# Decay attention into a squared-gate MLP on one core: a planner that may choose the engine of eight kinds of instruction, and float32 scores of two heads on the two halves of the rows

## The chip, the cores and the metric

The kernel runs on one core of one Trainium2 chip. Its time is the device time of one execution in microseconds (us); lower is better. The engines are PE (TensorE, matrix products; PEld is its weight load), DVE (VectorE), ACT (ScalarE), POOL (GpSimd) and SP (SyncE, which here only issues DMAs).

## The reference

Attention with a decay for 8 batches, 8 heads, 576 positions and 64 channels a head, and then a two-layer MLP over the 4608 tokens (512 to 2048 to 512) whose gate is quadratic between -1 and 1 and linear above:

```python
scores = np.matmul(q, k.transpose(0, 1, 3, 2)) / np.sqrt(D)
cum = np.cumsum(np.log(np.clip(f, 0.0001, 1.0)), axis=-1)
decay = cum[:, :, :, None] - cum[:, :, None, :]
scores = np.where(causal, -1000000000.0, scores + decay)   # causal: above the diagonal
attn = np.exp(scores - np.max(scores, axis=-1, keepdims=True))
attn = attn / (np.sum(attn, axis=-1, keepdims=True) + 1e-09)
x = np.matmul(attn, v)           # then to [B * S, H * D]
h = x @ w_in
g = np.where(h >= 1, h, np.where(h <= -1, 0.0, (h + 1) ** 2 / 4))
out = g @ w_out
```

## The kernel before

**Attention** goes by jobs: one pair of heads of one batch, or for batch 0 a part of it (rows of blocks 0 and 1, then blocks 2 to 4), 36 jobs in all. A job takes the rows of its 576 positions in blocks of 128 (the fifth has 64; there the two heads share one tile, head 0 on partitions 0 to 63 and head 1 on 64 to 127). For each block and head POOL writes decay and mask into a row buffer `sdr` or `sd` (lines 884 and 888), PE writes the scores into one of three PSUM tiles `s`, DVE adds both and takes the minimum (906), ACT takes the exponential and its sum (915), POOL adds the small constant to the sum (921), DVE inverts it (927). Row buffers are a ring of four, and one `sd`.

The first 12 jobs (`p < NQK`) compute scores in float32: PE turns q and k (694), ACT copies them from PSUM to `qkT` (700 and 705), and PE multiplies (713). q is copied twice, head 0 into the upper 64 partitions of one tile and head 1 into the lower 64 of another, the other halves being zero, so that each product reads all 128 rows against the k of both heads. Each float32 product is two instructions in the trace. The first 8 jobs (`p < NPE`) also turn the probabilities on PE, with a diagonal of inverse sums (`pr<-ident`, 937) as the second operand (957, 963), copied from PSUM by ACT (973).

The later jobs split each number into a high and a low half of float16: the high half is written by ACT with a scale and the low half by DVE as a difference. So are q and k (`qs`, 759 and 763; 767 and 773), v (`vs`, 805 and 811), the probabilities (`pr`, 989 and 992). Probabilities and q, k are turned by DMA; the scores are 795, the products with v 846.

**The MLP** goes by 18 chunks of 256 tokens and 8 double blocks of the hidden width (144 steps). Per step: 24 or 48 products into a PSUM tile `ph` (1055), ACT adds and squares into `u` (1064, 1067), DVE bounds it (1068), ACT writes the high half of `g` (1071), DVE the low half (1074), PE multiplies both with the second weights into `po` (1082). After the last step ACT scales two `po` tiles into `ot` (1098) and issues their DMAs. There are three `ph`, two `u`, three `g`. The weights are split once, in the first 200 us; the low half of the first matrix is made by POOL (524, 527), of the second by DVE (531).

**The order of the work** is a plan. Each piece of work is recorded with an engine, an estimated time, what it reads and writes, and a priority. `plan` then walks through estimated time and gives each free engine its first ready piece by priority, granting buffers as it goes, and the pieces are written out in that order. On the chip every engine runs its own list strictly in order. `A`, `V`, `G` and `M` record work for ACT, DVE, POOL and PE, so that the engine of a piece is fixed where it is recorded. `od.hold` keeps job ji from starting before 100 + 27 (ji - 8) us of planned time.

Of the kernel before, what the change touches and what calls it, by code (L numbers as in the profile page):

```python
# [9 lines left out]
F32 = mybir.dt.float32  # L10
# [61 lines left out]
class Order:  # L72
# [3 lines left out]
    def __init__(self):  # L76
        self.ops = []
        self.last = {}
        self.readers = {}
# [3 lines left out]
    def op(self, eng, dur, emit, reads=(), writes=(), prio=0.0, size=0.0, mode=0):  # L83
        i = len(self.ops)
        deps = set()
        bufs = set()
# [7 lines left out]
        for x in list(reads) + list(writes):  # L94
            b = x[0] if isinstance(x, tuple) else x
            if isinstance(b, Buf):
                bufs.add(b)
# [14 lines left out]
    def plan(self):  # L112
# [15 lines left out]
        for i in range(n):  # L128
            if not missing[i]:
                waiting[ops[i][0]].append(i)  # L130
# [6 lines left out]
        while done < n:  # L137
# [5 lines left out]
            while again:  # L143
                again = False
                for eng, l in waiting.items():
# [4 lines left out]
                    for i in l:  # L150
                        if ready[i] > t + 1e-9:
                            continue
# [34 lines left out]
                    l.remove(i)  # L187
# [31 lines left out]
                    for j in follow[i]:  # L219
                        missing[j] -= 1  # L220
                        same = ops[j][0] == eng and not size
                        late = SLACK if ops[j][0] == "PE" else 0.0
                        ready[j] = max(ready[j], free[eng] if same else after + late)
                        if not missing[j]:
                            k = (ops[j][5], j)
                            w = waiting[ops[j][0]]
                            lo, hi = 0, len(w)
                            while lo < hi:
                                mid = (lo + hi) // 2
                                if (ops[w[mid]][5], w[mid]) < k:  # L230
                                    lo = mid + 1
                                else:
                                    hi = mid
                            w.insert(lo, j)
                            if ready[j] > t:
                                heapq.heappush(events, ready[j])
# [21 lines left out]
def kernel(  # L258
# [119 lines left out]

    def M(us, emit, reads=(), writes=(), prio=0.0, mode=0):
# [45 lines left out]
    for i in range(1):  # L425
        G(0.3, lambda i=i: nc.gpsimd.memset(sd4_pool.cands[i][1][:, S:SP], 0.0), [], ["sdz"], -7.0)
    early_qk = {
        c: t[:, 0:6 * S].bitcast(F32).rearrange("p (c s) -> p c s", c=3) for c, t in qkt_pool.aps.items()
    }
    for c, t in early_qk.items():  # L430
        for h in range(2):
            G(0.6, lambda t=t, h=h: nc.gpsimd.memset(t[64 - 64 * h:128 - 64 * h, h, :], 0.0), [], ["qz"], -8.5)
# [51 lines left out]
    def weight_split(i, prio):  # L484
# [29 lines left out]
        for j in range(2):  # L514
# [8 lines left out]
            if j == 0:  # L523
                G(1.4, lambda wf=wf, s=s: nc.gpsimd.tensor_scalar(
                    out=wf, in0=wf, scalar1=s, scalar2=0.0, op0=ALU.mult, op1=ALU.add
                ), [("sw", i)], key, prio)
                G(2.6, lambda wf=wf, hi=hi, lo=lo: nc.gpsimd.tensor_tensor(
                    out=lo, in0=wf, in1=hi, op=ALU.subtract
                ), [], key + [("pl", i, j)], prio)
            else:  # L530
                V(1024, lambda wf=wf, hi=hi, lo=lo, s=s: nc.vector.scalar_tensor_tensor(
                    out=lo, in0=wf, scalar=s, in1=hi, op0=ALU.mult, op1=ALU.subtract
                ), [("sw", i)], key + [("pl", i, j)], prio)
# [91 lines left out]
    def attention(ji):  # L625
# [47 lines left out]
        if p < NQK:  # L673
# [9 lines left out]
            for j in range(2):  # L683
                part, _, keys = x32[j]
                n_all = s1 - (0 if j else s0)
                for a0 in range(0, n_all, 384):
# [10 lines left out]
                    if j == 0:  # L697
                        for h in range(2):
                            rows = slice(64 * h, 64 * h + 64)
                            A(n, lambda rows=rows, h=h, n=n, a0=a0, pt=pt: nc.scalar.activation(  # L700
                                view()[rows, h, a0:a0 + n], pt.ap[rows, 0:n], AF.Copy
                            ), [pt, "qz"], [(qt, h, a0)], pq)
                            qtkeys[h].append((qt, h, a0))
                    else:
                        A(n, lambda n=n, a0=a0, pt=pt: nc.scalar.activation(
# [467 lines left out]
```

## Time and profile before

| | us |
|---|---|
| median of 3 runs (range) | 1134.03 (1130.76 to 1135.49) |
| profiled execution, own time | 1131.35 |
| its span | 1129.6 |
| PE busy in it | 1053.3 (93%) |
| DVE, ACT, POOL busy | 800.5 (71%), 796.7 (71%), 478.8 (42%) |
| mean granted clock of PE | 0.981 |

The span is the time from the first to the last instruction that the profile shows; 1.75 us of the execution lie outside it. Busy times of an engine overlap with those of the others. A busy PE need not be PE at its peak, since the ends of its products are modelled.

### The profile page before, as it was taken

The numbers are of one execution on the slowest core, as the hardware profiler recorded it, in microseconds if no ns is written. First come the engines' busy times: TensorE is split into PE (matmuls) and PEld (weight loads), VectorE is DVE, ScalarE is ACT, GpSimd is POOL, SyncE is SP. The second block draws the span as 40 slices with busy tenths as digits, with TensorE's granted clock in tenths as the row PEclk, the third lists the DMA queues.
The fourth block names the chain that finished last, engine by engine and source line by source line (L and its number), as shares of the span: only waits on it lengthen the run. The fifth ranks groups of instructions, "written<-read, shape, count | busy, mean of one in ns | idle before, by whom it ended". The sixth has DMA issues, their size and how long they took to land. (4 is left out here: it accounts for less than half of the span.)

```text
span 1129.6 us, 24707 instructions
## 1 busy us (share of the span) xinstructions
PE 1053.3 (93%) x8805; PEld 708.8 (63%) x8805; DVE 800.5 (71%) x2156; ACT 796.7 (71%) x1667; POOL 478.8 (42%) x873
## 2 busy tenths in 40 slices
PE   4689788999999999999999999999999999999998
PEld 2445555556665666666666666666666667676675
DVE  5795888878878887887778878788787873322322
ACT  4566776776888887878787877788787974444443
POOL 4868863354554444444543543445434640000000
PEclk9689998999999999999999999999999999999999
DMA  7844444567779788768896987789868662000000
GB/s 195 284 149 104 151 127 111 103 120 152 149 165 179 144 168 154 160 136 166 164 170 141 170 147 160 145 171 170 145 133 153 138 120 41 17 21 11 10 19 19
DMA packets 390619, 146.37 MB, mean 130 GB/s; under 512 B 367328, under 2 KB 368352, under 8 KB 390496
## 3 DMA queue, kind: packets, MB, share of 16 engines
q1 hardware_dynamic: 385312, 135.35, 59.3%
q10 hardware_dynamic: 5184, 9.44, 2.4%
q8 instruction: 69, 1.13, 0.4%
q14 instruction: 54, 0.44, 0.1%
HBM read 65.68 MB, written 9.58 MB: 67 GB/s over the span
## 5 line engine op out<-in xcount | busy, mean ns | idle before, releaser
L1055 PE MATMUL ph<-x,place 128*128 128x256 f16 (+3 forms) x4608 | 407.0, 247 | 4.5 <-DVE x L863 1.4
L1082 PE MATMUL po<-place,g 128*128 128x512 f16 x1728 | 403.8, 381 | 2.6 <-ACT g L1071 2.3
L1055 PEld LDWEIGHTS <-place 128*128 128x128 f16 x4608 | 355.7, 98 | 55.3 <-issue 8.4
L1082 PEld LDWEIGHTS <-g 128*128 128x128 f16 x1728 | 164.1, 98 | 185.7 <-issue 5.2
L884 POOL TENSOR_SCALAR sdr<-ck,sg,cqs 128x128 f32<-128x128 f32 (+1 forms) x192 | 162.2, 845 | 201.2 <-DVE pr L992 180.4
L1068 DVE SCALAR_TENSOR_TENSOR u<-ph,z,u 128x512 f32<-128x512 f32 x144 | 107.4, 746 | 128.6 <-ACT u L1067 127.2
L915 ACT ACTIVATE sdr<-sdr,nm 128x512 f32<-128x512 f32 (+3 forms) x246 | 135.4, 551 | 52.9 <-DVE nm L906 34.2
L1064 ACT ACTIVATE u<-ph,z 128x512 f32<-128x512 f32 x144 | 110.4, 767 | 79.2 <-PE ph L1055 77.6
L1074 DVE SCALAR_TENSOR_TENSOR g<-u,z,g 128x512 f16<-128x512 f32 x144 | 113.6, 789 | 40.6 <-ACT g L1071 40.0
L989 ACT ACTIVATE pr<-sdr,nm 128x128 f16<-128x128 f32 (+1 forms) x224 | 114.3, 550 | 38.7 <-issue 23.6
L1071 ACT ACTIVATE g<-u,z 128x512 f16<-128x512 f32 x144 | 103.1, 716 | 53.1 <-DVE u L1068 52.4
L992 DVE SCALAR_TENSOR_TENSOR pr<-sdr,nm,pr 128x128 f16<-128x128 f32 (+1 forms) x224 | 115.8, 551 | 4.9 <-ACT pr L989 4.6
L906 DVE CUSTOM_DVE_ANT_0 sdr<-s,sdr,sg 128x128 f32<-128x128 f32 (+1 forms) x192 | 101.7, 541 | 22.2 <-POOL sdr L888 20.4
L795 PE MATMUL s<-qkT 128*128 128x128 f16 (+5 forms) x576 | 92.8, 297 | 11.2 <-DVE nm L906 6.7
L888 POOL TENSOR_SCALAR_AFFINE_SELECT sdr<-sdr 128x128 f32<-128x128 f32 x246 | 91.6, 372 | 18.1
L1067 ACT ACTIVATE u<-u 128x512 f32<-128x512 f32 x144 | 90.6, 629 | 4.2
L921 POOL TENSOR_SCALAR nm<-nm 128x2 f32<-128x2 f32 (+1 forms) x160 | 41.0, 256 | 93.8 <-ACT sdr L915 62.0
L846 PEld LDWEIGHTS <-vs 128*64 128x64 f16 x1176 | 58.6, 110 | 29.1 <-issue 23.8
L846 PE MATMUL s<-pT,vs 128*64 128x320 f16 (+4 forms) x1176 | 68.1, 263 | 9.1 <-DVE nm L906 5.9
L713 PE MATMUL s<-qkT 128*128 128x128 f32 (+5 forms) x192 | 64.4, 484 | 7.6 <-DVE nm L906 6.9
L795 PEld LDWEIGHTS <-qkT 128*128 128x128 f16 (+1 forms) x576 | 42.6, 101 | 42.5 <-issue 21.9
L884 POOL TENSOR_SCALAR sd<-ck,sg,cqs 64x576 f32<-64x576 f32 x48 | 42.2, 879 | 50.3 <-DVE pr L992 46.3
(138 smaller groups left out, 1129.3 us busy)
## 6 DMA issues: line engine op xcount, KB each, us to landing
ck<-cum_d SPq DMA_DIRECT2D x62, 288.0 KB, 3.7
out_dram<-ot ACTq DMA_DIRECT2D x36, 256.0 KB, 3.1
v<-in_v_dram SPq DMA_DIRECT2D x64, 128.0 KB, 3.2
qk<-in_k_dram SPq DMA_DIRECT2D x64, 128.0 KB, 3.0
qkT<-qkT SPq DMA_DIRECT2D x48, 160.0 KB, 3.5
qk<-in_q_dram SPq DMA_DIRECT2D x56, 128.0 KB, 3.1
place<-in_moe_w_in_dram SPq DMA_DIRECT2D x10, 512.0 KB, 4.9
place<-in_moe_w_out_dram SPq DMA_DIRECT2D x8, 512.0 KB, 6.3
```

The source lines that it names most:

```text
L795: nc.tensor.matmul(sp[p0:p1, 0:c1 - c0], lhsT=tq[:, h, q0 - s0:q0 - s0 + p1 - p0], rhs=tk[:, h, c0:c1], start=(c == 0), stop=(c == 1),)
L846: nc.tensor.matmul(av.ap[64 * h:64 * h + 64, c0:n], lhsT=vs.ap[:, vl, h, t, :], rhs=pT.ap[:, t, pl, h, c0:n], start=(t == 0 and pi == 0), ...
L884: nc.gpsimd.tensor_scalar(out=sd.ap[p0:p1, 0:wid], in0=cks[h].ap[p0:p1, 0:wid], scalar1=ns if p < NQK else ns[p0:p1], scalar2=cqs()[p0:p1, ...
L915: A(wid, lambda i=i, sd=sd, wid=wid, nm=nm, sm=sm: nc.scalar.activation(sd.ap[:, 0:wid], sd.ap[:, 0:wid], AF.Exp, bias=nm.ap[:, i:i + 1], ...
L989: A(cols, lambda i=i, prv=prv, rows_=rows_, rc=rc: nc.scalar.activation(prv()[:, :, 0, i, :], rows_(), AF.Copy, scale=rc.ap[:, i:i + 1]), ...
L992: V(cols, lambda i=i, prv=prv, rows_=rows_, rc=rc: nc.vector.scalar_tensor_tensor(out=prv()[:, :, 1, i, :], in0=rows_(), scalar=rc.ap[:, i ...
L1055: nc.tensor.matmul(ph.ap[:, fi * TC + a0:fi * TC + a1], lhsT=wi[fb][:, wl, t, fi * P:(fi + 1) * P], rhs=xs[b][:, t, xl, s0:s0 + a1 - a0], ...
L1064: A(512, lambda i=i, ph=ph, u=u: nc.scalar.activation(u.ap, ph.ap, AF.Relu, scale=z.u[:, i:i + 1], bias=z.h[:, i:i + 1]), [ph, z.key], [u] ...
L1068: V(512, lambda i=i, ph=ph, u=u: nc.vector.scalar_tensor_tensor(out=u.ap, in0=ph.ap, scalar=z.t[:, i:i + 1], in1=u.ap, op0=ALU.max, op1=AL ...
L1071: A(512, lambda i=i, u=u, g=g: nc.scalar.activation(g.ap[:, 0], u.ap, AF.Copy, scale=z.r[:, i:i + 1]), [u, z.key], [(g, 0)], pf - 1e4, 1)
L1074: V(512, lambda i=i, u=u, g=g: nc.vector.scalar_tensor_tensor(out=g.ap[:, 1], in0=u.ap, scalar=z.r[:, i:i + 1], in1=g.ap[:, 0], op0=ALU.mu ...
L1082: nc.tensor.matmul(po.ap[i], lhsT=g.ap[:, gl, fi * TC + i * P:fi * TC + (i + 1) * P], rhs=wo[fb][:, wl, fi, :], start=(fb == first and fi ...
```

## The change

1. `op` takes a list `other` of further engines, each with its own estimated time, and `plan` puts such a piece in the waiting list of each of them; the first engine that is free when the piece is ready and its buffers can be had takes it. `X` records such pieces. Their eight kinds, with the engines in the order listed (A is ACT, D is DVE, G is POOL): q and k out of PSUM (AD), high halves of q and k (AG), of v (AG), of the probabilities (AG) and of `g` (AG), the diagonal (GDA), the turned probabilities out of PSUM (AD), the first scaling of `po` into `ot` (AD). The low half of both weights (POOL or DVE) and the small constant on the sum (POOL or DVE) are recorded in the same way by `op`.
2. In the first 12 jobs q is copied once, as k is. The product of head h reads rows 64h to 64h+63 alone, and the products of both heads stand next to each other in one piece `both`, which needs the PSUM tiles of both heads at once. The two zero fills of each `qkT` buffer on POOL (four `MEMSET`) are gone.
3. The set of buffers of a piece becomes a dict, so that its order is that of recording.

```diff
+    def op(self, eng, dur, emit, reads=(), writes=(), prio=0.0, size=0.0, mode=0, other=()):
+        if other:
+            self.other[i] = {e: (us, late) for e, us, late in other}
...
-                waiting[ops[i][0]].append(i)
+                for e in (ops[i][0], *self.other.get(i, ())):
+                    waiting[e].append(i)
...
-                    l.remove(i)
+                    if i in self.other:
+                        for e in (ops[i][0], *self.other[i]):
+                            waiting[e].remove(i)
+                        if eng != ops[i][0]:
+                            ops[i][0:2] = eng, self.other[i][eng][0]
+                    else:
+                        l.remove(i)
...
+    def times(eng, out, in_, scale):
+        if eng == "ACT":
+            nc.scalar.activation(out, in_, AF.Copy, scale=scale)
+        elif eng == "DVE":
+            nc.vector.tensor_scalar(out=out, in0=in_, scalar1=scale, scalar2=None, op0=ALU.mult)
+        else:
+            nc.gpsimd.tensor_scalar(out=out, in0=in_, scalar1=scale, scalar2=0.0, op0=ALU.mult, op1=ALU.add)
...
+    def X(n, emit, reads=(), writes=(), prio=0.0, engs="AG", ptr=1, late=0.0):
+        us = {"A": ("ACT", act_us(n, ptr)), "D": ("DVE", dve_us(n)), "G": ("POOL", pool_us(n))}
+        (first, t), *rest = [us[c] for c in engs]
+        op(first, t, emit, reads, writes, prio, other=[(e, u, late) for e, u in rest])
...
             def product(h, sp, p0, p1, q0, c0, c1):
                 t = view()
                 nc.tensor.matmul(
-                    sp[p0:p1, 0:c1 - c0], lhsT=t[:, h, q0 - s0:q0 - s0 + p1 - p0], rhs=t[:, 2, c0:c1], start=True, stop=True,
+                    sp[p0:p1, 0:c1 - c0], lhsT=t[64 * h:64 * h + 64, 0, q0 - s0:q0 - s0 + p1 - p0],
+                    rhs=t[64 * h:64 * h + 64, 1, c0:c1], start=True, stop=True,
                 )
...
+                    def both(ci=ci, q0=q0, c0=c0, c1=c1, sps=sps, r=r):
+                        for h in range(2):
+                            if r < LAST:
+                                product(h, sps[h][ci].ap, 0, P, q0, c0, c1)
+                            else:
+                                product(h, sps[0][ci].ap, 64 * h, 64 * h + 64, q0, c0, c1)
...
-            A(512, lambda i=i, u=u, g=g: nc.scalar.activation(
-                g.ap[:, 0], u.ap, AF.Copy, scale=z.r[:, i:i + 1]
-            ), [u, z.key], [(g, 0)], pf - 1e4, 1)
+            X(512, lambda e, i=i, u=u, g=g: times(
+                e, g.ap[:, 0], u.ap, z.r[:, i:i + 1]
+            ), [u, z.key], [(g, 0)], pf - 1e4)
```

Counted over the whole program, the written order has these instructions on the engines (products and DMAs are the same in number; the new lines are 393 and 401 on ACT, 395 and 403 on DVE, 397 on POOL, 953 for the sum, 556 and 557 for low weight halves on POOL, 731 for the float32 scores):

| kind | before | after |
|---|---|---|
| high half of `g` | ACT 144 | ACT 41, POOL 103 |
| high half of `pr` | ACT 252 | ACT 133, POOL 119 |
| high halves of `qs`, `vs` | ACT 76 | ACT 33, POOL 43 |
| constant on the sum | POOL 160 | POOL 75, DVE 85 |
| diagonal | POOL 36 | POOL 13, ACT 14, DVE 9 |
| first `ot` | ACT 36 | ACT 18, DVE 18 |
| `pT` out of PSUM | ACT 32 | ACT 23, DVE 9 |
| `qkT` out of PSUM | ACT 52 | ACT 25, DVE 11 |
| low half of a weight | POOL 8 pairs, DVE 8 | POOL 6 pairs, DVE 10 |

PE in the first float32 scores of block 3, early in the program, where `s` are the PSUM tiles of scores, `ph` those of turned operands, `pr` a diagonal. Before, the products of the two heads of block 2 of the second pair stand apart:

```order
L713 MATMUL s_65<-qkT_107 128x384
L957 MATMUL ph_68<-pr_100,pr_103 128x128 x4
L957 MATMUL ph_70<-pr_100,pr_103 128x128 x2
L713 MATMUL s_66<-qkT_107 128x384
L694 MATMUL ph_69<-ident,qk_0_89 128x128 x2
```

In the changed program the two heads of a block stand next to each other, here of block 3 and of the last one, 64 rows a head:

```order
L731 MATMUL s_65<-qkT_106 128x512
L731 MATMUL s_67<-qkT_106 128x512
L731 MATMUL s_66<-qkT_106 64x512 x2
L447 MATMUL ph_68<-dg_150,ones 128x2
L434 MATMUL ph_69<-ident,ms_152 2x128
```

What moved is that nothing stands between the two heads of a block any more, and that they take different rows of the array; a product of another shape comes behind them.

POOL in the middle of the program, where it makes decay rows (884, 888). Before, its list holds these and the small sums:

```order
L884 TENSOR_SCALAR sdr_98<-ck_112,sg_173,cqs_170 128x384
L888 AFFINE_SELECT sdr_98<-sdr_98 128x128
L884 TENSOR_SCALAR sdr_95<-ck_114,sg_173,cqs_170 128x512
L888 AFFINE_SELECT sdr_95<-sdr_95 128x128
L921 TENSOR_SCALAR nm_131<-nm_129 128x2
L884 TENSOR_SCALAR sdr_96<-ck_112,sg_173,cqs_170 128x512
L888 AFFINE_SELECT sdr_96<-sdr_96 128x128
```

After, at about the same place, the decay rows are 901 and 905, and high halves stand between them:

```order
L397 TENSOR_SCALAR pr_103<-sdr_96,nm_124 128x4x128
L397 TENSOR_SCALAR g_119<-u_116,z_153 128x512
L901 TENSOR_SCALAR sdr_96<-ck_112,sg_175,cqs_172 128x256
L905 AFFINE_SELECT sdr_96<-sdr_96 128x128
L901 TENSOR_SCALAR sdr_95<-ck_113,sg_175,cqs_172 128x256
L905 AFFINE_SELECT sdr_95<-sdr_95 128x128
L953 TENSOR_SCALAR nm_126<-nm_130 128x1
L397 TENSOR_SCALAR pr_104<-sd_0_99,nm_126 128x5x128
```

A decay row now waits behind high halves in POOL's list, and a high half behind decay rows.

ACT, in the same stretch. Before, each step of the MLP has three instructions there:

```order
L1064 ACTIVATE u_115<-ph_70,z_155 128x512
L1067 ACTIVATE u_115<-u_115 128x512
L1071 ACTIVATE g_118<-u_115,z_155 128x512
L1064 ACTIVATE u_116<-ph_69,z_155 128x512
L1067 ACTIVATE u_116<-u_116 128x512
```

After, some steps have two, and where DVE has one of the `ot` tiles, ACT's DMA issue of that tile still stands in ACT's list:

```order
L1095 ACTIVATE u_116<-ph_69,z_155 128x512
L1098 ACTIVATE u_116<-u_116 128x512
L947 ACTIVATE sdr_96,nm_129<-sdr_96,nm_126 128x512
L947 ACTIVATE sdr_95,nm_129<-sdr_95,nm_126 128x512
L879 ACTIVATE x_80<-s_65 128x256
L393 ACTIVATE ot_0_120<-po_71,z_155 128x512
L1134 DMA out_dram<-ot_0_120 128x512
L1134 DMA out_dram<-ot_1_121 128x512
```

The high half of `g` has left ACT in that step, and the issue of `ot_1` now waits for DVE.

More of the change, by code (lines that the diff above doesn't have):

```diff
@@ L77, in __init__ @@
         self.ops = []
+        self.other = {}
         self.last = {}
@@ L96, in op @@
             if isinstance(b, Buf):
-                bufs.add(b)
+                bufs[b] = None
         for x in reads:
@@ L150, in plan @@
                     for i in l:
-                        if ready[i] > t + 1e-9:
+                        if (ready[i] if ops[i][0] == eng else ready[i] + self.other[i][eng][1]) > t + 1e-9:
                             continue
@@ L220, in plan @@
                         missing[j] -= 1
-                        same = ops[j][0] == eng and not size
+                        same = ops[j][0] == eng and not size and j not in self.other
                         late = SLACK if ops[j][0] == "PE" else 0.0
@@ L225, in plan @@
                             k = (ops[j][5], j)
[L226 to L236, printed above, removed]
+                            for e in (ops[j][0], *self.other.get(j, ())):
+                                w = waiting[e]
+                                lo, hi = 0, len(w)
+                                while lo < hi:
+                                    mid = (lo + hi) // 2
+                                    if (ops[w[mid]][5], w[mid]) < k:
+                                        lo = mid + 1
+                                    else:
+                                        hi = mid
+                                w.insert(lo, j)
+                                late = ready[j] + (self.other[j][e][1] if e != ops[j][0] else 0.0)
+                                if late > t:
+                                    heapq.heappush(events, late)
         self.start = start
@@ L522, in weight_split, with low @@
             ), key + [("sw", i)], [("pl", i, j)], prio, 1)
[L523 to L533, printed above, removed]
+            def low(e, wf=wf, hi=hi, lo=lo, s=s):
+                if e == "DVE":
+                    nc.vector.scalar_tensor_tensor(out=lo, in0=wf, scalar=s, in1=hi, op0=ALU.mult, op1=ALU.subtract)
+                else:
+                    nc.gpsimd.tensor_scalar(out=wf, in0=wf, scalar1=s, scalar2=0.0, op0=ALU.mult, op1=ALU.add)
+                    nc.gpsimd.tensor_tensor(out=lo, in0=wf, in1=hi, op=ALU.subtract)
+            op("POOL", 3.5, low, [("sw", i)], key + [("pl", i, j)], prio, other=[("DVE", 1.46, 0.0)])
     def load_values(b, hp, prio):
@@ L696, in attention @@
                     M(0.26 * -(-n // P), turn, keys, [pt], pq)
[L697 to L705, printed above, removed]
[L706 to L709 removed]
+                    X(n, lambda e, j=j, n=n, a0=a0, pt=pt: copy(
+                        e, view()[:, j, a0:a0 + n], pt.ap[:, 0:n]
+                    ), [pt], [(qt, j, a0)], pq, "AD", 0)
+                    for l in qtkeys:
+                        l.append((qt, j, a0))
             def product(h, sp, p0, p1, q0, c0, c1):
@@ L924, in inverse @@
                 )
-            G(0.2, inverse, [(sm, i) for i in range(nh)], [rc], pw)
+            op("POOL", 0.26, inverse, [(sm, i) for i in range(nh)], [rc], pw, other=[("DVE", 0.22, 0.0)])
             V(0, lambda rc=rc, nh=nh: nc.vector.reciprocal(rc.ap[:, 0:nh], rc.ap[:, 0:nh]), [], [rc], pw, 0.25)
```

82 lines of the change are left out of this document (42 added, 40 removed).

## The prediction

> **What bounds the kernel now.** I read the page's busy shares first, then the busy time by stage, then who waits for whom in each stage, and last the groups that the edits touch.
>
> ```profile
> span 1129.6 us, 24707 instructions
> ...
> PE 1053.3 (93%) x8805; PEld 708.8 (63%) x8805; DVE 800.5 (71%) x2156; ACT 796.7 (71%) x1667; POOL 478.8 (42%) x873
> ...
> core 0: us, PE busy (x) PEld busy (x) DVE busy (x) ACT busy (x) POOL busy (x), PEclk, DMA share, GB/s
> 0.00:50.00 50.00, 27.04 (x114) 18.10 (x116) 30.88 (x78) 25.67 (x63) 31.88 (x72) 0.83 0.84 252
> 50.00:280.00 230.00, 204.98 (x1329) 130.62 (x1328) 186.04 (x487) 160.39 (x336) 133.38 (x209) 0.95 0.52 127
> 280.00:940.00 660.00, 636.47 (x5852) 433.71 (x5850) 531.27 (x1522) 532.62 (x1155) 313.52 (x592) 1.00 0.81 154
> 940.00:1129.00 189.00, 184.79 (x1517) 126.33 (x1515) 52.33 (x71) 78.00 (x114) 0.00 (x0) 1.00 0.04 15
> ```
>
> PE is the bound. It idles 23 us of the first 50, 25 us of the next 230 (the float32 jobs and the weights), 23.5 us of the middle 660, and 4 us of the last 189, where only the MLP is left. MLP work can fill PE whenever it is ready, so a microsecond of PE work or idle time taken out early shortens the last stage. At most 76 us of idle time and the float32 work itself are to be had. The change can do nothing in the last stage but lengthen it.
>
> **The float32 scores.** Their groups, and three stretches of PE's timeline around 76 and 104 us:
>
> ```profile
> L713 PE MATMUL s<-qkT 128*128 128x512 f32 x32 | 17.6, 642 | 0.2 <-DVE nm L906 0.2
> L713 PE MATMUL s<-qkT 128*64 128x512 f32 x32 | 13.5, 675 | 2.5 <-DVE nm L906 2.5
> L713 PE MATMUL s<-qkT 128*128 128x256 f32 x32 | 12.9, 499 | 3.7 <-DVE nm L906 3.1 <-DVE x L863 0.4
> L713 PE MATMUL s<-qkT 128*128 128x384 f32 x32 | 12.7, 505 | 0.5 <-DVE nm L906 0.4
> L713 PE MATMUL s<-qkT 128*128 128x128 f32 x32 | 7.4, 337 | 0.8 <-DVE nm L906 0.8
> L713 PE MATMUL s<-qkT 128*64 128x64 f32 x32 | 3.8, 244 | 0.0
> ...
> 76.22 1.98 PE L713 MATMUL s<-qkT 128*128 128x512 f32 x4
> ...
> 78.14 1.08 PE L713 MATMUL s<-qkT 128*64 128x512 f32 x4
> ...
> 104.67 1.07 PE L713 MATMUL s<-qkT 128*64 128x512 f32 x2
> ```
>
> The three stretches are the argument. Two heads of 512 columns on the whole array are four instructions and take 1.98 us. The last block's heads use half of the columns each (128*64): standing together, four take 1.08 us; with other work between them, one head's two take 1.07. So two tiles of the array do run side by side, also in float32, when their products stand together. No product here uses half of the rows, so that halves of rows behave like halves of columns is taken over from this row. Then the four groups of 128*128 (17.6 + 12.9 + 12.7 + 7.4 = 50.6 us) shrink by 0.90 of 1.98, which is 45%: 23 us. The last blocks (17.3 us) gain only where heads stood apart: eight blocks, each 1.08 for the wide and, by the same ratio, 0.3 for the narrow products, would be 11 us; I take 4 of the 6 us.
>
> Against it stands the changing of shape: counted along PE's list, products of one shape follow those of another 188 times before and 257 times after. The price of one change is bounded by nothing and by a weight load that no product hides:
>
> ```profile
> L713 PEld LDWEIGHTS s<-qkT x192: 132/189/338, 15.7 to 271.6; 128*128 128x128 f32 x128, 128*64 128x64 f32 x64
> ```
>
> Half of its median of 189 ns, 0.1 us, times 69 is 7 us. Net: 23 + 4 - 7 = 20 us of PE work. Bounds: a gain of 29, and with no overlap a loss of up to 13. PE is busy for 89% of 50 to 280, DVE for 81%, and both wait for each other, so not all of it becomes time. What is late next is DVE, whose scores (906) free the PSUM tiles; and `both` needs two of the three tiles at once, where a head alone needed one. I count 11 of the 20 us.
>
> **Other early work.** PE's waits from 50 to 280 us, the largest and those that the edits touch (us in total, times, longest), and the low half of a weight on DVE (ns, least, median and most):
>
> ```profile
> PE ph L963 <- POOL pr L937: 3.3, 2, 2.7
> PE s L713 <- DVE nm L906: 3.3, 4, 2.5
> PE ph L694 <- ACT qkT L700: 2.9, 2, 2.0
> ...
> PE ph L957 <- POOL pr L937: 2.5, 3, 1.1
> ...
> L531 DVE SCALAR_TENSOR_TENSOR place<-place,sw,place x4: 1285/1340/2397, 32.0 to 149.0; 128x1024 f16<-128x1024 f32 x4
> ```
>
> The diagonal (3.3 + 2.5) is what POOL delays now and what ACT or DVE can now take; the copies to `qkT` (2.9) are 16 fewer and shared with DVE. Together 9 us, of which I count 4: DVE, to which 9 diagonals, 20 copies and 2 low halves of weights come, is the busier engine. Ends: 9 gained, or 5 lost, if the 2 low halves (1.34 us each) and some copies stand ahead of the scores' DVE work. The zero fills on POOL stand before the first product, which waits for a DMA: nothing.
>
> **The middle.** What moves there, by rows of the middle stretch (those of L921 and L989 are of the whole span):
>
> ```profile
> L1071 ACT ACTIVATE g<-u,z 128x512 f16<-128x512 f32 x93 | 66.4, 714 | 21.0 <-DVE u L1068 20.5
> L884 POOL TENSOR_SCALAR sdr<-ck,sg,cqs 128x512 f32<-128x512 f32 x48 | 47.1, 982 | 40.2 <-DVE pr L992 39.2
> L884 POOL TENSOR_SCALAR sd<-ck,sg,cqs 64x576 f32<-64x576 f32 x48 | 42.2, 879 | 50.3 <-DVE pr L992 46.3 <-DVE nm L927 1.7
> L805 ACT ACTIVATE vs<-v,sv 128x640 f16<-128x640 f32 x23 | 18.8, 816 | 0.0
> ...
> L989 ACT ACTIVATE pr<-sdr,nm 128x128 f16<-128x128 f32 (+1 forms) x224 | 114.3, 550 | 38.7 <-issue 23.6
> ...
> L921 POOL TENSOR_SCALAR nm<-nm 128x2 f32<-128x2 f32 (+1 forms) x160 | 41.0, 256 | 93.8 <-ACT sdr L915 62.0
> ...
> PE s L795 <- DVE nm L906: 6.7, 13, 1.1
> PE s L846 <- DVE nm L906: 5.1, 10, 1.0
> ...
> DVE nm L927 <- POOL nm L921: 31.7, 44, 2.0
> DVE u L1068 <- ACT u L1067: 23.0, 33, 3.0
> DVE sdr L906 <- POOL sdr L888: 20.4, 37, 1.1
> ```
>
> POOL has no such instruction before, so its price is that of 884 at the same width: 0.98 us for 512 columns against ACT's 0.71, and 0.9 as a mean of all widths. Of 265 high halves on POOL 38 of `g` stand behind the last decay row, in the last stage. Of the other 227 some 85% (24 of 28 float16 jobs) lie in the middle: 193 at 0.9 are 174 us, and some 70 sums fewer, at 0.256, take off 18. POOL goes from 313 to about 469 of 660 us (71%). ACT loses the same 193 at 0.65, the mean of its rows here weighted by the counts, and a few `ot`: from 533 to about 401 (61%). DVE, with the sums and `ot`, goes from 531 to about 555 (84%).
>
> PE waits there mostly for DVE to free `s` (6.7 + 5.1). DVE in turn waits 31.7 us for the small sum on POOL, which it can now make itself, 23.0 for ACT's square, which stands behind fewer high halves, and 20.4 for decay rows, which stand behind more. Two of these waits shrink and one grows; I take nothing for PE's idle time here. Ends: 10 gained (nearly all of the 11.8), 15 lost (the second rival).
>
> **The last stage.** 38 high halves of `g` at 0.98 instead of 0.71 are hidden behind PE, but not the last two, which the chain of waits shows at the end; the two `ot` run side by side on ACT and DVE:
>
> ```profile
> 1118.94 0.72 ACT g L1071
> ...
> 1121.81 0.73 ACT g L1071
> 1122.59 2.56 PE po L1082 x11
> ...
> 1125.76 0.68 ACT ot L1098
> ```
>
> Plus 0.5, minus 0.7: nothing. In the middle, ACT's issue of `ot_1` waits for DVE and holds ACT's list; 18 times at most one DVE instruction (0.8 us) on an engine with 40% free: nothing, while that room lasts.
>
> **Sum.** 11 + 4 = 15 us. Against the profiled execution's 1131.35 that is 1116; the median of the runs lies 2.7 above that execution, so I forecast 1119.
>
> **A rule beside a row.** The Trainium skill, "TensorEngine Tiling (Array Packing)", Gotcha 1: PSUM Pressure, says that tiles on different rows cannot use the same PSUM bank at a time. Blocks 0 to 3 write the two heads to two tiles `s`, the last block writes both to one. By the rule the last blocks would run one head after the other; the trace shows two heads writing one tile together (the 1.08 us), but on different columns, not rows. The fourth rival works out its price from those rows.
>
> Another page, "GPSIMD Engine Reference", section 1, says that POOL shares its path to the on-chip memory with DVE, with contention when DVE reads two operands from there. These rows show who pays:
>
> ```profile
> L1074 DVE SCALAR_TENSOR_TENSOR g<-u,z,g 128x512 f16<-128x512 f32 x93 | 72.7, 782 | 12.4 <-ACT g L1071 11.9
> ...
> L1074 DVE SCALAR_TENSOR_TENSOR g<-u,z,g 128x512 f16<-128x512 f32 x32 | 24.0, 751 | 25.3 <-ACT g L1071 25.3
> ...
> L884 POOL TENSOR_SCALAR sdr<-ck,sg,cqs x188: 450/757/2364, 292.6 to 926.6; 128x384 f32<-128x384 f32 x48, 128x512 f32<-128x512 f32 x48, 128x128 f32<-128x128 f32 x46, 128x256 f32<-128x256 f32 x46
> ```
>
> DVE's low half of `g` takes 782 ns in the middle and 751 in the last stage, where POOL is idle; POOL's decay rows spread from 450 to 2364 ns. So POOL pays, and the 0.98 above holds that already.
>
> **Rivals.**
> 1. The middle improves too. ACT and DVE wait less in the chain of `g` and of the sums, and PE's waits for `s` nearly vanish: 10 more, 1109; with a fuller gain early (29 instead of 11) down to 1100. For it: the 31.7 and 23.0 us. Against it: DVE at 84%. Chance 0.2.
> 2. POOL becomes the late engine: slower. A decay row stands behind one or two high halves of 0.9 us, DVE's list stops at 906, and PE's products wait for `s`. It decides where DVE's waits for decay rows go from 20 us beyond about 70: DVE then has no room (555 + 70 of 660) and the rest falls on PE, some 25 us after the early gain of 15: 1144. At half of that it is 1131. For it: the 2364 ns and the 71%. Against it: POOL now idles more than half of the middle. Chance 0.13 slower, 0.1 near 1131.
> 3. Halves of rows do not overlap, so that the edit on the scores does not do what it says: 4 us gained early, 7 lost by changes of shape, 1134 + 3 = 1137. No row here shows the contrary. Chance 0.1.
> 4. The last blocks' heads do not overlap, being in one bank: instead of 4 us gained, eight blocks lose 1.98 - 1.08 in the wide and 0.2 in the narrow products, 9 us, half of it on the path: with the lost gain 6 us, 1125. Chance 0.1.
>
> The forecast itself has 0.37. A change of 0.5%, 5.7 us, is about what a measurement of this kernel can tell from none, so 1128.4 and 1139.7 are the limits. Faster: the forecast, rivals 1 and 4, a few of the others, 0.67. Same: half of rival 2 and most of 3, 0.19. Slower: the other half of 2, 0.14. The range leaves out the deep end of rival 1 and the end of rival 2: 1102 to 1138.
>
> **What the profile will show.** If right: the float32 groups fall from 67.9 us in the sum of the six rows to about 46, with four instructions of 512 columns in some 1.1 us; PE idles no more than 24 us from 280 to 940; POOL stands near 71% there, and its high halves of 512 columns near 0.98 us. If wrong: DVE's waits for decay rows are several times 20 us, or PE waits for POOL's `g`. What I cannot see is how long POOL takes to write float16 into strided blocks (`pr`, `qs`); at 1.5 times the price taken POOL would pass 80%, and rival 2 holds.

## The result, and the profile after

The changed kernel takes 1142.11 us (median of 4 runs, 1140.83 to 1143.26), the kernel before 1132.39 beside it: a ratio of 1.0084, with a 95% interval of 1.006 to 1.0107. It is slower by 0.8%, where 1119 was forecast, 1.3% under the 1134.03 of before. The profiled execution's span went from 1129.6 to 1141.5 us.

The totals of the page and the busy time by stage, as shown of before (PE, PEld, DVE, ACT and POOL busy in us, the granted clock, the DMA share and GB/s):

```profile
span 1141.5 us, 24980 instructions
PE 1054.6 (92%) x8805; PEld 701.1 (61%) x8805; DVE 860.5 (75%) x2290; ACT 628.5 (55%) x1362; POOL 631.7 (55%) x1022
...
0.00:50.00 50.00, 29.18 (x117) 19.15 (x119) 34.86 (x90) 22.01 (x52) 21.98 (x55) 0.91 0.83 252
50.00:280.00 230.00, 206.44 (x1393) 126.26 (x1391) 204.31 (x553) 142.12 (x308) 149.84 (x225) 0.92 0.57 133
280.00:940.00 660.00, 622.50 (x5649) 420.61 (x5646) 559.81 (x1567) 408.45 (x922) 432.89 (x706) 0.99 0.79 151
940.00:1141.00 201.00, 196.48 (x1656) 135.06 (x1653) 61.49 (x83) 55.97 (x80) 26.99 (x38) 1.00 0.07 18
```

The loss is in the middle. PE idles 37.5 of its 660 us, where it idled 23.5, and finishes 5649 products there instead of 5852; what was not done is done after 940, in a last stage that is 12 us longer. DVE, which with ACT had been the busiest beside PE, went from 531 to 560 us (85%).

The start is earlier, as forecast. The float16 scores (line 795, now 813), with first and last start at the end of the times:

```profile
L795 PE MATMUL s<-qkT x576: 189/302/403, 283.1 to 928.1; 128*128 128x128 f16 x48, 128*128 128x512 f16 x48, 128*64 128x512 f16 x26, 128*128 128x256 f16 x24
```

```profile
L813 PE MATMUL s<-qkT x576: 189/322/521, 271.0 to 936.7; 128*128 128x128 f16 x48, 128*128 128x512 f16 x48, 128*64 128x512 f16 x25, 128*128 128x256 f16 x24
```

The first of them starts 12.1 us earlier, the last 8.6 us later. So 21 us are lost between the two.

The six groups of float32 scores after, and two stretches of PE's timeline:

```profile
L731 PE MATMUL s<-qkT 64*128 64x512 f32 x32 | 11.0, 703 | 0.0
L731 PE MATMUL s<-qkT 64*128 64x256 f32 x32 | 10.7, 533 | 3.1 <-DVE nm L938 3.0
L731 PE MATMUL s<-qkT 64*64 64x512 f32 x32 | 9.5, 672 | 1.2 <-DVE nm L938 1.2
L731 PE MATMUL s<-qkT 64*128 64x384 f32 x32 | 9.3, 583 | 0.0
L731 PE MATMUL s<-qkT 64*128 64x128 f32 x32 | 6.4, 407 | 1.8 <-DVE nm L938 1.0 <-DVE qkT L403 0.7
L731 PE MATMUL s<-qkT 64*64 64x64 f32 x32 | 2.7, 242 | 0.4 <-DVE nm L938 0.4
```

```profile
76.66 1.13 PE L731 MATMUL s<-qkT 64*128 64x512 f32 x4
...
78.97 1.07 PE L731 MATMUL s<-qkT 64*64 64x512 f32 x4 [1.18 <-DVE nm L938]
```

Together 49.6 us instead of 67.9. Four instructions of 512 columns take 1.13 us where they took 1.98; the four of the last block, both heads in one tile, take 1.07.

The waits of the middle that answer to those of before (us, times, longest), and the one long wait of PE:

```profile
DVE u L1099 <- ACT u L1098: 14.9, 18, 3.8
DVE pr L1023 <- POOL pr L397: 11.6, 14, 2.1
DVE g L1105 <- POOL g L397: 11.2, 21, 0.9
DVE nm L959 <- POOL nm L953: 9.1, 12, 1.5
PE s L813 <- DVE nm L938: 8.6, 18, 1.0
...
DVE sdr L938 <- POOL sdr L905: 6.0, 17, 0.9
PE s L813 <- DMA qkT<-qkT: 5.8, 3, 4.5
...
PE po L1113 <- ACT g L393: 3.7, 6, 1.6
PE po L1113 <- POOL g L397: 3.3, 5, 1.4
```

The last two answer to this one of before:

```profile
PE po L1082 <- ACT g L1071: 0.2, 1, 0.2
```

```profile
517.27 0.90 PE L813 MATMUL s<-qkT 128*128 128x128 f16 x5 [4.50 <-DMA qkT<-qkT]
```

DVE waits less for small sums (31.7 to 9.1), for squares (23.0 to 14.9) and for decay rows (20.4 to 6.0). New are its waits for POOL's high halves, 22.8 us. They stand largely in place of others: before, DVE waited 25.2 us for ACT's high halves of `g` and `pr`, and now 9.0, so that the two engines together make it wait 31.8. PE's waits for DVE's sums and minima to free `s` are no longer in total than before, 11.8 us (8.6 + 3.2, and 6.7 + 5.1). What grew are its waits for the high halves of `g` in front of the second product, 7.0 us (3.3 for POOL's, 3.7 for ACT's) instead of 0.2, which is half of the growth of its idle time; that PE waits for POOL's `g` was one of the prediction's signs of being wrong. The DMA wait of 4.5 us stands in a stretch (500 to 525 us) where the granted clock is 0.86. Such waits need no high half on POOL: they come to 8.0 and 8.1 us in two runs below that have none there (scores alone, and high halves on ACT, both with the delay of 100).

DVE's low halves in the middle, before (two rows; that of `g` stands in the prediction) and after, and POOL's high half of `g`:

```profile
L992 DVE SCALAR_TENSOR_TENSOR pr<-sdr,nm,pr 128x384 f16<-128x384 f32 x48 | 28.0, 612 | 0.3 <-ACT pr L989 0.2
...
L992 DVE SCALAR_TENSOR_TENSOR pr<-sdr,nm,pr 128x256 f16<-128x256 f32 x48 | 21.2, 480 | 0.1
```

```profile
L1105 DVE SCALAR_TENSOR_TENSOR g<-u,z,g 128x512 f16<-128x512 f32 x88 | 73.8, 838 | 17.9 <-POOL g L397 11.2 <-ACT g L393 6.5
...
L1023 DVE SCALAR_TENSOR_TENSOR pr<-sdr,nm,pr 128x384 f16<-128x384 f32 x48 | 31.3, 681 | 0.6 <-POOL pr L397 0.6
L1023 DVE SCALAR_TENSOR_TENSOR pr<-sdr,nm,pr 128x256 f16<-128x256 f32 x48 | 26.4, 580 | 1.8 <-ACT pr L393 1.3 <-POOL pr L397 0.4
```

```profile
L397 POOL TENSOR_SCALAR g<-u,z 128x512 f16<-128x512 f32 x52 | 43.3, 832 | 47.6 <-DVE u L1099 37.7 <-DVE m L583 5.3 <-DVE nm L953 2.2
```

The same instruction on DVE got longer: `g` 782 to 838 ns, `pr` of 384 columns 612 to 681, of 256 columns 480 to 580 (that of 640 columns did not, 887 to 891). The trace also tells the low halves of `g` apart by how much of each one's time POOL was busy as well. Where it was under a fifth, they take 746 ns before (36 of them) and 743 after (24); where it was over four fifths, 817 (47) and 860 (43).

### The profile page after: what moved, and what is told of

Same layout as the page of the kernel before. It is cut to its first block, busy times and chain, and to the rows that moved or that the text cites. A ratio compares the mean times of both kernels' runs of the same rounds, so it can differ in the third digit from the quotient of the medians.

```text
span 1141.5 us, 24980 instructions
## 1 busy us (share of the span) xinstructions
PE 1054.6 (92%) x8805; PEld 701.1 (61%) x8805; DVE 860.5 (75%) x2290; ACT 628.5 (55%) x1362; POOL 631.7 (55%) x1022
## 3 DMA queue, kind: packets, MB, share of 16 engines
q8 instruction: 69, 1.13, 0.4%
## 5 line engine op out<-in xcount | busy, mean ns | idle before, releaser
L397 POOL TENSOR_SCALAR g<-u,z 128x512 f16<-128x512 f32 x103 | 83.8, 814 | 241.6 <-DVE u L1099 228.3
L901 POOL TENSOR_SCALAR sdr<-ck,sg,cqs 128x128 f32<-128x128 f32 (+1 forms) x192 | 155.2, 808 | 65.0 <-DVE pr L1023 58.7
L1105 DVE SCALAR_TENSOR_TENSOR g<-u,z,g 128x512 f16<-128x512 f32 x144 | 116.5, 809 | 53.0 <-POOL g L397 46.1
L1023 DVE SCALAR_TENSOR_TENSOR pr<-sdr,nm,pr 128x128 f16<-128x128 f32 (+1 forms) x224 | 127.1, 598 | 5.2 <-POOL pr L397 2.4
L393 ACT ACTIVATE pr<-sdr,nm 128x128 f16<-128x128 f32 (+3 forms) x126 | 66.8, 546 | 69.9 <-issue 27.1
L905 POOL TENSOR_SCALAR_AFFINE_SELECT sdr<-sdr 128x128 f32<-128x128 f32 x246 | 94.1, 383 | 18.1
L397 POOL TENSOR_SCALAR pr<-sdr,nm 128x384 f16<-128x384 f32 (+3 forms) x98 | 59.5, 609 | 36.7 <-DVE nm L959 23.1
L863 PE MATMUL s<-pT,vs 128*64 128x320 f16 (+4 forms) x1176 | 67.9, 263 | 6.7 <-DVE nm L938 4.2
L731 PE MATMUL s<-qkT 64*128 64x128 f32 (+5 forms) x192 | 49.1, 523 | 6.5 <-DVE nm L938 5.7
```

The costliest lines, as they stand in the source:

```text
L397: nc.gpsimd.tensor_scalar(out=out, in0=in_, scalar1=scale, scalar2=0.0, op0=ALU.mult, op1=ALU.add)
L863: nc.tensor.matmul(av.ap[64 * h:64 * h + 64, c0:n], lhsT=vs.ap[:, vl, h, t, :], rhs=pT.ap[:, t, pl, h, c0:n], start=(t == 0 and pi == 0), ...
L901: nc.gpsimd.tensor_scalar(out=sd.ap[p0:p1, 0:wid], in0=cks[h].ap[p0:p1, 0:wid], scalar1=ns if p < NQK else ns[p0:p1], scalar2=cqs()[p0:p1, ...
L1023: V(cols, lambda i=i, prv=prv, rows_=rows_, rc=rc: nc.vector.scalar_tensor_tensor(out=prv()[:, :, 1, i, :], in0=rows_(), scalar=rc.ap[:, i ...
L1105: V(512, lambda i=i, u=u, g=g: nc.vector.scalar_tensor_tensor(out=g.ap[:, 1], in0=u.ap, scalar=z.r[:, i:i + 1], in1=g.ap[:, 0], op0=ALU.mu ...
```

## The experiments

Theory A (in the later expectations "contention"): the parts of the change have fixed effects, and what costs is the high halves on POOL, which make DVE late. Theory B ("plan scatter"): any edit makes the planner draw another order, and some orders are bad by themselves. Theory C: the paired scores, which need two `s` tiles at once, delay the middle.

**The parts apart.** The edit on the scores with every kind on the engine of before; the free choice with the scores of before; and the changed kernel with the high halves of q, k, v, `pr` and `g` all kept on ACT. Each is the changed kernel with lines of these kinds (an `X` with one letter, or `op` without `other`):

```diff
 scores_only: all eight kinds; high_fixed: only those that write a high half
-            ), [u, z.key], [(g, 0)], pf - 1e4)
+            ), [u, z.key], [(g, 0)], pf - 1e4, "A")
 choice_only: the zero fills and the products of before in place of `both`
-            if p < NQK:
+            if False:
```

> Every piece stays on its engine of before; only the float32 scores read half of the rows a head and stand in pairs, with q copied once. Theory A (DVE is the late engine: the high halves on POOL slow the low halves on DVE, and DVE has new work besides): the early stretch keeps its gain of some 9 us and the middle is as before: about 1123. Theory B (any change of the plan moves the middle by up to 10 us, whatever it is): anywhere from 1115 to 1140. Theory C (the paired scores themselves delay the middle): 1130 or more.

> The whole choice of engines, with the float32 scores of before (all 128 rows, a head at a time). Theory A: the loss of the middle without the gain of the scores: about 1150. Theory B: anywhere from 1125 to 1155. Theory C: 1132, as before.

> The changed kernel with the high halves of q, k, v, the probabilities and g all on ACT; sums, first ot, diagonals, copies and low weight halves stay free. Theory A: DVE's low halves are back at their durations of before (128x384 at 612 ns, not 681), DVE keeps sums and ot: 1125 to 1130. If the sums and ot on DVE alone are the cause: 1140. Theory B: 1120 to 1140.

Measured: scores alone 1142.82 (ratio to before 1.0085, 1.0051 to 1.0118), choice alone 1147.78 (1.0136, 1.0117 to 1.0154), high halves on ACT 1124.36 (0.9921, 0.9903 to 0.9938). The last two are about what A expects. But the scores alone lose as much as the whole, and neither A nor a sum of parts allows that; it speaks for B or C. The choice alone lies 16 us over what C expects of it.

**The same kernels, another drawing.** `HOLD` is the 100 us of `od.hold`. One microsecond of it changes no work, only the order that the planner draws and, where it has a choice, some of the engines (in the changed kernel POOL has 1028, 1022 and 997 instructions with 99, 100 and 101).

```diff
-HOLD, PACE = 100.0, 27.0
+HOLD, PACE = 101.0, 27.0
```

> The kernel before with the jobs' earliest planned start put off by 1 us: another plan of the same work on the same engines. Theory A (what a part of the change does belongs to that part): 1132, within 3 us. Theory B (the plan's order decides, and any change of the plan's input draws it anew): within 8 us of 1132, but more than 3 away about half of the time.

> The paired scores alone, put off by 1 us. Theory A: 1143, as scores_only without the delay. Theory B: the early gain of some 8 us stands and the middle is drawn anew: more likely 1122 to 1136 than 1143.

> The changed kernel with the jobs' earliest planned start put off by 1 us (101 + 27 (ji - 8)), which makes another plan of the same work on the same choice of engines. Theory A: within 3 us of the changed kernel, 1142. Theory B: off by more than 4 us either way, with no cause in the engines' load.

> The changed kernel with the earliest planned start 1 us sooner. Theory A: 1142, within 3 us. Theory B: 1130 to 1146.

> The changed kernel with the high halves on ACT, put off by 1 us. Theory A: 1124, within 3 us. Theory B: 1118 to 1136.

> All high halves on ACT, and the delay of the jobs 99 instead of 100 us: a third drawing of the order of this version (1124.4 with 100, 1114.9 with 101). Contention: 1110 to 1127, under every drawing of the changed kernel itself (1131.6, 1135.3, 1142.1). Plan scatter alone: a mean over the three drawings as for the changed kernel, so this one near 1140 or above.

> A third drawing of the order of the kernel before (delay of the jobs 99 instead of 100). With 1132.4 (100) and 1137.2 (101) known: 1130 to 1140. It gives the mean of three drawings of before, against which the versions' means are set.

> A third drawing of the edit on the scores alone. 1142.8 (100) and 1130.2 (101) are known. If the edit gains the 11 us that the prediction gave it, hidden by one bad drawing: 1118 to 1128. If the early gain is lost again in the middle whatever the drawing: 1130 to 1143.

Medians in us, by the delay:

| version | 99 | 100 | 101 | mean |
|---|---|---|---|---|
| before | 1129.5 | 1132.4 | 1137.2 | 1133.0 |
| scores alone | 1125.0 | 1142.8 | 1130.2 | 1132.7 |
| changed kernel | 1131.6 | 1142.1 | 1135.3 | 1136.4 |
| changed, high halves on ACT | 1110.8 | 1124.4 | 1114.9 | 1116.7 |

Both are true. B: one kernel moves by 8 to 18 us with its drawing, 6.6 us as a standard deviation within a row, so that a mean of three is known to about 3.8 and a difference of two means to about 5.4. By that the scores alone gain 0.3 +- 5.4, and the changed kernel loses 3.4 +- 5.4 to before: of the 9.7 us measured, the means bear out a third, and the rest may be the drawing. A: the high halves on POOL cost 19.7 +- 5.4, and every drawing of the version without them is faster than every drawing of the changed kernel; taken delay by delay the difference is 20.8, 17.7 and 20.4. C falls with 1125.0, and with 1130.2, which is 7 us under before at the same delay. The best is all high halves on ACT with a delay of 99: 1110.75 us, 0.981 of before (0.9769 to 0.9852).

PE's idle time in the middle (660 us less its busy time, from one profiled execution each) goes the same way:

| version | 99 | 100 | 101 | mean |
|---|---|---|---|---|
| before | 17.7 | 23.5 | 19.4 | 20.2 |
| scores alone | 18.2 | 31.6 | 27.0 | 25.6 |
| changed kernel | 28.0 | 37.5 | 30.1 | 31.9 |
| changed, high halves on ACT | 17.2 | 22.4 | 19.4 | 19.6 |

So the loss of the middle is there in every drawing of the changed kernel, and gone with the high halves back on ACT. Between the last two rows the waits of PE itself that the traces show fall, as means, from 30.4 to 18.8 us: by 4.9 where the second product waits for `g`, by 3.9 where DVE's sums and minima have to free `s`, and by less elsewhere.

**Which high halves.** Only those of `g` kept on ACT, and only those of q, k, v and `pr`, both with the delay of 100.

```diff
 g_fixed
-            ), [u, z.key], [(g, 0)], pf - 1e4)
+            ), [u, z.key], [(g, 0)], pf - 1e4, "A")
 att_fixed (and likewise qs and vs)
-                    ), kk + [rc], [(prb, i)], pw + 0.5)
+                    ), kk + [rc], [(prb, i)], pw + 0.5, "A")
```

> The changed kernel with the high half of g always on ACT, all else free. If the 103 high halves of g are what costs (they are written just when DVE writes the low half of another step): about 1128, four fifths of the way to the 1124 of the kernel with all high halves on ACT. If it is the attention's high halves (119 of pr, 43 of qs and vs): about 1138. If only the order drawn counts: anywhere from 1130 to 1145, with DVE's durations no guide.

> The changed kernel with the high halves of q, k, v and of the probabilities always on ACT, that of g free. Mirror of the run before: about 1138 if g is what costs, about 1128 if it is the attention's halves. Contention says the gain over 1142 goes with DVE's busy time in the middle (560 us with all on POOL, about 535 with none, plus the sums).

1123.5 (0.9926, 0.9895 to 0.9956) and 1126.4 (0.9946, 0.9922 to 0.9971). Either half of the cut brings nearly all of it, where each branch of the expectations had one of the two near 1128 and the other near 1138; with the scatter above, no kind can be named as the culprit.

**The order held fixed.** To take the drawing out, the plan stays as it is and only the engine of an instruction changes when it is written out. First the changed kernel's order, with POOL's high halves issued on ACT where ACT was a choice:

```diff
-        od.ops[i][2](od.ops[i][0]) if i in od.other else od.ops[i][2]()
+        od.ops[i][2]("ACT" if od.ops[i][0] == "POOL" and "ACT" in (od.first[i], *od.other[i]) and od.first[i] == "ACT" else od.ops[i][0]) if i in od.other else od.ops[i][2]()
```

> The plan and the written order are those of the changed kernel (1142), but each high half that the plan gave to POOL is issued on ACT, at the same place in the program. Contention (POOL's high halves slow DVE's low halves where both work): the low halves fall back to the durations of before (g 838 to about 780 ns, pr of 384 681 to about 612, in the middle), DVE's middle falls from 560 to about 540 us although its list is the same, and the time falls to 1125 to 1133, less what ACT now is late (its busy time rises from 408 to about 535 of 660). Plan scatter alone (the drawn order is bad, whichever engine writes the halves): 1142 or more, since the order is the same and ACT has 125 us more to do.

It took 1148.89 (1.0145, 1.0098 to 1.0193). Middle stage, and the rows of DVE:

```profile
280.00:940.00 660.00, 620.61 (x5543) 416.20 (x5543) 537.82 (x1567) 511.36 (x1114) 280.43 (x515) 0.99 0.79 151
```

```profile
L1107 DVE SCALAR_TENSOR_TENSOR g<-u,z,g 128x512 f16<-128x512 f32 x88 | 66.8, 759 | 16.1 <-ACT g L395 15.4
...
L1025 DVE SCALAR_TENSOR_TENSOR pr<-sdr,nm,pr 128x384 f16<-128x384 f32 x48 | 27.9, 611 | 0.0
L1025 DVE SCALAR_TENSOR_TENSOR pr<-sdr,nm,pr 128x256 f16<-128x256 f32 x48 | 22.5, 499 | 3.1 <-ACT pr L395 2.8
```

```profile
DVE pr L1025 <- ACT pr L395: 20.8, 29, 1.1
DVE g L1107 <- ACT g L395: 15.4, 26, 1.3
...
PE po L1115 <- ACT g L395: 7.9, 13, 1.3
```

The durations fell back (838 to 759, 681 to 611, 580 to 499) and DVE's middle by 22 us with the same list. So the lengthening goes with POOL's high halves. Yet the time did not fall: ACT, with 103 us more in an order made for two engines, was late instead. DVE waits 36.2 us for its high halves, and PE 7.9 for those of `g`. The durations came as contention has it, and the time (1125 to 1133 by contention, 1142 or more by plan scatter) as plan scatter has it.

Then the reverse: the best order (1110.75), with the high halves of `g`, or of `pr`, issued on POOL.

```diff
 high_order_g (high_order_pr likewise, in the piece of pr)
-                e, g.ap[:, 0], u.ap, z.r[:, i:i + 1]
+                "POOL", g.ap[:, 0], u.ap, z.r[:, i:i + 1]
```

> The plan and order of the best version (all high halves planned on ACT, delay 99: 1110.8), but the 144 high halves of g are issued on POOL at the same place. ACT loses 66 us in the middle (526 to about 460 of 660), POOL gets 77 (295 to about 372), DVE's list is unchanged. Contention: DVE's low halves of g rise from 755 to 820 or more ns, DVE's middle by 6 to 10 us, and the time by 5 to 12 us (1116 to 1123), though the engine that was relieved was busier than the one that got the work. Plan scatter alone: no loss, 1105 to 1113, since the order is that of 1110.8 and ACT waits less.

> The same with the high halves of the probabilities on POOL in place of g (some 215 in the middle, 134 us at the 746, 738, 514, 373 and 880 ns that they took there): ACT's middle 526 to about 402, POOL's 295 to about 430 (65%). Contention: low halves of pr up by 5 to 15%, and decay rows now behind them, 1118 to 1130. Plan scatter alone: 1105 to 1115.

1147.05 (1.0131, 1.007 to 1.0191) and 1150.6 (1.0154, 1.0103 to 1.0205): 36 and 40 us lost at an unchanged order, though ACT, which was relieved, had been far busier than POOL. Both theories had less (1123 at most for `g`, 1130 for `pr`). Middle stage, waits and low halves, first of the best version (its profiled execution is the slowest of its four, 1114.95), then of `g` on POOL, then of `pr` on POOL:

```profile
280.00:940.00 660.00, 642.81 (x5936) 436.81 (x5934) 544.31 (x1586) 526.00 (x1139) 294.62 (x526) 1.00 0.81 152
```

```profile
DVE g L1108 <- ACT g L393: 11.5, 22, 0.8
DVE pr L1026 <- ACT pr L393: 7.8, 11, 1.5
PE s L816 <- DVE nm L941: 5.0, 10, 1.2
```

```profile
L1108 DVE SCALAR_TENSOR_TENSOR g<-u,z,g 128x512 f16<-128x512 f32 x93 | 70.2, 755 | 11.8 <-ACT g L393 11.5
...
L1026 DVE SCALAR_TENSOR_TENSOR pr<-sdr,nm,pr 128x256 f16<-128x256 f32 x48 | 21.7, 488 | 0.0
```

```profile
280.00:940.00 660.00, 623.22 (x5592) 416.74 (x5590) 542.64 (x1586) 465.01 (x1041) 374.31 (x619) 1.00 0.81 153
```

```profile
POOL g L397 <- DVE u L1102: 65.5, 37, 9.4
DVE g L1108 <- POOL g L397: 35.2, 40, 2.2
...
PE s L816 <- DVE nm L941: 14.7, 24, 1.6
PE po L1116 <- POOL g L397: 6.3, 12, 1.5
```

```profile
L1108 DVE SCALAR_TENSOR_TENSOR g<-u,z,g 128x512 f16<-128x512 f32 x89 | 66.7, 750 | 35.5 <-POOL g L397 35.2
```

```profile
280.00:940.00 660.00, 619.51 (x5585) 418.63 (x5584) 558.37 (x1585) 417.04 (x910) 431.03 (x747) 1.00 0.80 151
```

```profile
DVE pr L1026 <- POOL pr L397: 38.7, 45, 2.2
...
PE s L816 <- DVE nm L941: 14.0, 23, 1.3
PE s L866 <- DVE nm L941: 11.5, 12, 2.3
```

```profile
L1026 DVE SCALAR_TENSOR_TENSOR pr<-sdr,nm,pr 128x256 f16<-128x256 f32 x48 | 24.8, 542 | 13.3 <-POOL pr L397 13.3
```

With `pr` on POOL the slowing is there (488 to 542 ns; DVE 544 to 558 us). With `g` on POOL it is not: 755 to 750 ns, where 820 was expected, and DVE's busy time is the same; still 36 us are gone. No high half on POOL runs beside these low halves; the low halves of `pr` of 512 columns, beside which some run, went from 755 to 778. What both share is the wait: DVE stands at a low half until POOL has written the high one (11.5 to 35.2 us; 7.8 to 38.7), the scores behind it come late, and PE waits for them (at line 816 from 5.0 to 14.7 and 14.0, and with `pr` on POOL at line 866 too, 11.5). With `g` on POOL, PE also waits 6.3 us for the high half itself (1116). POOL waits 65.5 us for `u` in front of `g`, with its other work queued behind. So a late high half costs by itself, without a slower low half of `g`. As in the run before, the instructions were issued against the plan, so 36 us is probably more than a planned move would cost; between the planned versions it was 19.7 for all kinds. The granted clock does not sort these versions: the profiled execution of the scores alone with the delay of 99 took 1120.2 us at a mean of 0.971, that of `g` on POOL 1147.2 at 0.990.

**What gains in the version of 1110.75.** Beside the scores alone (1125.0 with the delay of 99), all kinds but the high halves are free in it. DVE waits 30.6 us in the middle for POOL's small sum in the one and 7.1 in the other. With the delay of 99: only the sum free; and all but the sum and the high halves.

```diff
 sums_hold99: scores alone, but
-            op("POOL", 0.2, lambda inverse=inverse: inverse("POOL"), [(sm, i) for i in range(nh)], [rc], pw)
+            op("POOL", 0.26, inverse, [(sm, i) for i in range(nh)], [rc], pw, other=[("DVE", 0.22, 0.0)])
 nosums_hold99: high halves on ACT, and the same line the other way
```

> Delay 99. The edit on the scores, and of the eight kinds only the small constant on the sum free to go to DVE. Known with the same delay: 1125.0 with none of the eight free, 1110.8 with all but the high halves free. DVE waited 31 us for POOL's small sum without, 7 with. If that wait is what the freed kinds gain: 1110 to 1117, and DVE's waits for POOL's nm fall to about 8 us. If the others (copies out of PSUM, diagonal, low weight halves, ot) gain it: 1121 to 1128.

> The mirror, delay 99: as the version of 1110.8, but the small constant on the sum stays on POOL. If the sums are the gain: 1119 to 1127, with some 30 us of DVE's waits for POOL's nm back. If the others are: 1108 to 1115. If only the drawing counts, the two need not be mirrors of each other.

1130.51 (0.9974, 0.9953 to 0.9995) and 1133.36 (0.9999, 0.9985 to 1.0014): neither keeps the gain, and each lies over both ranges expected of it. Waits of the middle in the first:

```profile
DVE nm L970 <- POOL nm L964: 8.9, 16, 1.6
PE s L824 <- DMA qkT<-qkT: 8.3, 7, 2.3
```

The wait for the sum went as expected, to 8.9, and in the second it was back at 31.7, and the times did not follow; other waits came, such as 8.3 us for the DMA that turns q and k. Each of the two is a single drawing. Which of the freed kinds gives the 16.0 +- 5.4 us between the means of 1132.7 and 1116.7, or whether it takes several together, stays open.

## Why the prediction was wrong, step by step

- **Scores, 20 us of PE work:** right in mechanism, smaller in size. The four groups of 128*128 fell from 50.6 to 37.4 us, 13 instead of 23; the last blocks from 17.3 to 12.2, 5 instead of 4: together 18, where 27 gross and 20 net of the changes of shape were forecast. The share of 45% came from heads that stand together; one such pair did go from 1.98 to 1.13, but on average over the groups the gain is a quarter. What the 69 changes of shape cost is not separated from that. All of PE's work, though, gained less than its score groups: its busy time over the whole span is 1055.6 us before and 1045.4 with the scores alone, as means of three drawings, so about 10 of the 20 forecast.
- **Early sum, 15 us:** 12.1 by the start of the float16 jobs, and 9.2 as a mean over the three drawings (271.2 us instead of 280.4). But "a microsecond taken out early shortens the last stage" is not borne out: three drawings of the scores alone average 0.3 +- 5.4 us under before. They start the float16 scores 6 us earlier, and PE idles 5 us longer in the middle.
- **The middle, nothing:** this is the step that failed. It weighed three waits of DVE, and the high half itself, for which DVE and PE wait, was not among them. PE's idle time grew by 14 us, near the end of 15 lost, and by 10.3, 14.0 and 10.6 at the three delays. With the high halves on ACT it is no longer than before, so it is their place on POOL that costs it; in time that place costs 19.7 us. How much of this is the late high half and how much the slower DVE stays open. ACT (408 us, 401 forecast) and DVE (560, 555) came near the forecast, but DVE by another way. The sums and `ot` on it are some 23 us (24 forecast), and on top came low halves that take longer: 56 ns x 88 for `g`, 69 and 100 ns x 48 for the two forms of `pr` shown are 13 us; fewer MLP steps in the stage hide the rest in the sum.
- **"So POOL pays":** wrong, and the trace of before could have told: its low halves of `g` take 746 ns in the middle with POOL idle and 817 with POOL busy. The row behind it, 782 ns in the middle and 751 in the last stage, compared decay rows of POOL against one form on DVE, at half of POOL's later load. With 433 us of POOL work that form takes 838, and it is 759 when the work is taken off POOL at the same order. What the Trainium skill's "GPSIMD Engine Reference", section 1, says of contention where DVE reads two operands from the on-chip memory agrees with these rows; the low half of `g` and of `pr` read two, while DVE's bound on `u`, with one operand from PSUM, stayed at 745 ns.
- **POOL's price:** too high. 0.83 us for `g` instead of 0.98, and POOL was at 66% instead of 71%. A cheaper POOL took the work and still cost time.
- **The last stage:** nothing, and right, though the added 0.5 was not paid: the chain that ended last does hold one high half on POOL, in front of the last products, and it took no longer than ACT's before (0.73). The stage grew by what was left over from the middle.

```profile
1130.91 0.71 POOL g L397
```

- **Rival 2** gave the time (1144), but not by its mechanism: DVE's waits for decay rows fell to 6.0 us instead of passing 70. The late thing was the high half itself: DVE waited 31.8 us for high halves in the middle of its own list (25.2 before), and PE 7.0 for those of `g` (0.2 before). That its time comes within 2 us of the measured one is luck. **Rivals 3 and 4** are refuted by the 1.13 and the 1.07 us: row halves run together, also into one PSUM tile. By Gotcha 1 of the Trainium skill's "TensorEngine Tiling (Array Packing)" the last block's heads, on different rows, should have gone one after the other; here, on different rows and different columns, they did not. **Rival 1**, a middle that improves too, is nearest to the best drawing of the version without high halves on POOL (1110.8 against its 1109): PE idles 17.2 us there and DVE waits 7.1 for the small sum, but 45.5 for the squares, not less. Its deep end of 1100 does not follow from its own terms; 29 instead of 11 early gives 1091.
- **Missing altogether** was the scatter of the planner. An edit that redraws an order of thousands of pieces moves this kernel by some 6.6 us before its own effect counts; the range of 1102 to 1138 left no room for it on the far side of a loss.

## What to carry to other kernels

A free engine is not a free place for work whose result a busy, strictly ordered engine needs next: count the wait in that engine's list, and what the two do to each other's durations, before counting busy time moved. Where a planner sets the order, time a few neutral redrawings of both kernels before believing a difference of 1%, and compare means. A test at a fixed order shows what an instruction's place costs, but overstates a move that the planner would have planned for.

## What the runs showed of the hardware beyond that

Float32 products on two halves of the rows run together like those on two halves of the columns: four instructions of 512 columns in 1.13 us (two PSUM tiles) and 1.07 us (one tile, different partitions and columns of the array), against 1.98 on the whole array. POOL writes a float16 high half of 512 columns from float32 in 0.83 us, faster than its decay row of the same width (0.98 before, 0.88 beside it in the changed kernel). DVE's low halves, with two operands in the on-chip memory, took 7% longer for `g` and, for `pr`, from nothing (640 columns) to 21% longer (256 columns) beside a POOL that was 66% busy. With `g` on POOL at the best order (57% busy) those of `g` were no longer (750 ns), those of `pr` of 512 columns 3% longer. What goes with it is whether POOL is at work during the instruction: in `g`'s low halves of the changed kernel, 743 ns where it is hardly, 860 where it is nearly throughout.
